# Two sliding-window attentions: the V product no longer stands between the two halves of a step's logits

## The chip, the cores and the metric

The kernel runs on one core of one Trainium2 chip. The metric is device time in microseconds (us) from the start to the end of one execution; a profiled execution also has a span, from its first to its last instruction. The engines are TensorE (PE, with its weight loads PEld), VectorE (DVE), ScalarE (ACT), GpSimd (POOL) and SyncE (SP), which issues most of the DMAs. Each works through its own queue in order and waits on semaphores for the others.

## The reference

Four layers over 2048 rows of 576 values: attention, mixer, attention, mixer. Each adds its result to its input x. Cut to what matters here:

```python
x = x + A(layernorm(x)); x = x + B(layernorm(x)); x = x + A(layernorm(x)); x = x + B(layernorm(x))

def A(x, wqkv, wo):                 # 32 heads of 18 values
    q, k, v = split(x @ wqkv)
    # row s sees the rows s, s-2, ... s-14 (8 of them, those that exist)
    attn = softmax(q . k[window] * 18 ** -0.5)
    return (attn @ v[window]) @ wo

def B(x, w_in, w_sp, b_sp, w_out):  # 4608 = 2 x 2304
    z = gelu(x @ w_in)
    z1, z2 = z[:, :2304], layernorm(z[:, 2304:])
    return (z1 * (w_sp @ z2 + b_sp)) @ w_out
```

## The kernel before, in words

`layer_A` (from L322) is an attention, `layer_B` a mixer. In an attention the order of the work on every engine is written out by hand (`manual_schedule`): engines run their instructions in the order in which the Python code issues them. In the mixers a scheduler places them.

An attention cuts the 2048 rows into 19 tiles t of 112 rows, each with 16 earlier rows as its window's reach. A tile is worked on in two steps, one for each half of the heads, 38 steps s = 2t and 2t + 1 in all. The pieces are:

- `PG`: five products with 512 columns for a piece of Q or K, whose copy goes by DMA to the layout of the logits (`QK`).
- `VW(t, hh, dve)` (L375): the V product, five products of 288 columns for a half of the heads, into a small PSUM tile `pv`, and a cast to `v_ext` on DVE or ACT.
- `L_mm(s)` (L428): 16 logit products, 112 columns, with 32 rows of contraction (18 values of a head and 14 rows that add the mask of the window). They fill two PSUM tiles `L_ps`, `jp` 0 and 1. There are two such buffers, so each belongs to one half of a step (`H_tile`, L199).
- `EXP(s)` (L443): two exponentials on ACT, one per `L_ps` tile.
- `PV(s)` (L451): 16 products of the exponentials with V into one small PSUM tile `O_ps`; then on DVE a reciprocal and a multiplication, the softmax's division; after the second half of the heads a DMA transpose into `oT`.
- `WO(i, hh, c)` (L489): one product of the output projection, 288 columns. Five of them fill a small PSUM tile `pw`, which DVE adds to the old x; after ten, 128 rows are ready and `LN_STATS` (DVE), `LN_XN` (POOL), `XST` and `LN_T` (SP) prepare them for the mixer.

The small tiles `pv`, `O_ps`, `pw` and `pp` share four buffers (`PT_tile`, L202). A buffer is free again when its reader (DVE or ACT) is done.

A table holds for each step which `PG`, `VW` and later work it does. `wo_quota(s)` (L711) reads the table's costs of the step (1.08 us for a `PG`, 0.61 for a `VW`) and fills the step with output products up to 1.28 us of TensorE work in the first attention and 1.33 in the second, at 0.1215 each. What is left over goes to the next step, and `min(7.99, ...)` bounds it. `wo_run(s, n)` (L689) issues up to n of them, as far as the transposed rows are old enough (`wo_from`).

In step s the loop (L737 to L756) issues the logits and exponentials of step s + 1, then `PV(s)`, then the output products that complete a half-filled `pw`, then the table's work, then the rest of the output products. From step 14 (`PG_END`) there is a second form, for a step whose table holds a V product for the first half of the heads: it takes the V product out of the table and issues it between the two halves of the logits of step s + 1:

```python
L_mm(s + 1, (0,))
EXP(s + 1, (0,))
VW(*vws[0][1])
table[s].remove(vws[0])
L_mm(s + 1, (1,))
EXP(s + 1, (1,))
```

These V products are cast on DVE; those of the second half of the heads, in the steps between, are cast on ACT.

Of the kernel before, what the change touches and what calls it, by code (L numbers as in the profile page):

```python
# [62 lines left out]
class K:  # L63
# [258 lines left out]
    def layer_A(self, li):  # L322
# [32 lines left out]
        def tdim(t):  # L355
            nq = min(QT, S - QT * t)
            return HALO + nq, nq
# [11 lines left out]
        def evac(out, in_, dve):  # L369
            if dve:  # L370
                nc.vector.tensor_copy(out=out, in_=in_)  # L371
            else:
                nc.scalar.copy(out=out, in_=in_)

        def VW(t, hh, dve):  # L375
            nk = tdim(t)[0]
            pv = self.PT_tile([P, 512], f32, "pv")
            for c in range(5):
                nc.tensor.matmul(pv[:nk, 0:288], lhsT=self.xnT[:, c, QT * t:QT * t + nk],  # L379
                                 rhs=wv_sb[:, c, hh * 288:(hh + 1) * 288], start=(c == 0), stop=(c == 4))  # L380
            evac(v_ext[:nk, t, 16 * hh:16 * hh + 16, 0:DH], pv[:nk, 0:288].rearrange("p (b d) -> p b d", d=DH), dve)
# [43 lines left out]
        NST = 2 * NT  # L425
        L_tiles = {}

        def L_mm(s, jps=(0, 1)):  # L428
            t, hf = divmod(s, 2)
            nk, nq = tdim(t)  # L430
            if 0 in jps:
                L_tiles[s] = [self.H_tile("L_ps") for _ in range(2)]
            for jp in jps:
                for ftl in range(4):
                    g = 4 * hf + ftl
                    for jj in range(2):
                        j = 2 * jp + jj
                        nc.tensor.matmul(L_tiles[s][jp][:nk, jj, ftl * QT:ftl * QT + nq],  # L438
                                         lhsT=kT[32 * j:32 * j + 32, g, QT * t:QT * t + nk],
                                         rhs=qT[32 * j:32 * j + 32, g, QT * t + PADL:QT * t + PADL + nq],  # L440
                                         start=True, stop=True, tile_position=(32 * j, 0))

        def EXP(s, jps=(0, 1)):  # L443
            nk, nq = tdim(s // 2)
            for jp in jps:
                L_ps = L_tiles[s][jp]
                Lv = L_ps[:, :, 0:4 * QT].rearrange("p a (b c) -> p a b c", c=QT)
                nc.scalar.activation(out=P_bufs[(2 * s + jp) % 4][:nk, :, :, 0:nq], in_=Lv[:nk, :, :, 0:nq], func=ACT.Exp,  # L448
                                     scale=scale)

        def PV(s):  # L451
            t, hf = divmod(s, 2)
            nk, nq = tdim(t)
            O_ps = self.PT_tile([P, 512], f32, "O_ps")
            for jp in range(2):
                for ftl in range(4):
                    for jj in range(2):
                        idx = 4 * ftl + 2 * jp + jj
                        nc.tensor.matmul(O_ps[:, idx * (DH + 1):(idx + 1) * (DH + 1)],  # L459
                                         lhsT=P_bufs[(2 * s + jp) % 4][:nk, jj, ftl, :],  # L460
                                         rhs=v_ext[:nk, t, 16 * hf + idx, :], start=True, stop=True)
            Ov = O_ps[:, 0:16 * (DH + 1)].rearrange("p (h e) -> p h e", e=DH + 1)
            o_t = o_bufs[t % len(o_bufs)]
            rec = sb.tile([P, 16], f32, name="rec", tag="rec", bufs=2)
            nc.vector.reciprocal(out=rec[:nq, :], in_=Ov[:nq, :, DH])
            nc.vector.tensor_tensor(out=o_t[:nq, 288 * hf:288 * (hf + 1)].rearrange("p (h d) -> p h d", d=DH),  # L466
                                    in0=Ov[:nq, :, 0:DH], in1=rec[:nq, :, None].to_broadcast([nq, 16, DH]), op=ALU.mult)
            if hf == 1:
                c0 = (QT * t) % (RING * P)
                if t < NT - 2:  # L470
                    nc.sync.dma_start_transpose(out=oT[:, :, c0:c0 + nq], in_=o_t[:nq, :])
# [194 lines left out]
        table = {}  # L666
# [5 lines left out]
        PG_END = 14  # L672
# [16 lines left out]
        def wo_run(s, n):  # L689

            while n > 0 and wo_pos[0] < 10 * NS:
                i, m = divmod(wo_pos[0], 10)
                if s < wo_from[i]:
                    break
                if m == 0 and i % 2 == 0 and i + 2 < NS:
                    XO(i + 2)
                WO(i, m // 5, m % 5)
                wo_pos[0] += 1
                n -= 1
                if m == 9:  # L700
                    LN_STATS(i)
                    at(s + 1, LN_XN, i)
                    at(s + 1, XST, i)
                    if i < NS - 1:
                        k_ = s + 3
                        if li == 0 and i < 13:
                            k_ = max(k_, 19 + 2 * i if i < 8 else 35 + (i - 8) // 2)
                        at(k_, LN_T, i)
            return n

        def wo_quota(s):  # L711
            if s >= NST:
                return 10 * NS
            used = sum({PG: 1.08, VW: 0.61}.get(f, 0) for f, a in table.get(s, []))
            wo_due[0] = min(7.99, max(0, wo_due[0] % 1 + (wo_fill - used) / 0.1215))
            return int(wo_due[0])
# [10 lines left out]
        for k_, (d, qk, cc) in enumerate(pre):  # L727
            if k_ == (2 if li == 0 else 0):
                L_mm(0)
                EXP(0)  # L730
            PG(d, qk, cc, li > 0 or k_ < 4, q2)
            if li == 0 and k_ == 3:
                self.fill_window_rows(QK, 1)
# [1 line left out]
            VW(nvw - 1, 0, False)  # L735
            VW(nvw - 1, 1, False)
        for s in range(NST):  # L737
            n = wo_quota(s)
            vws = [e for e in table.get(s, []) if e[0] is VW]
            if s >= PG_END and s + 1 < NST - 2 and vws and vws[0][1][1] == 0:  # L740
                L_mm(s + 1, (0,))
                EXP(s + 1, (0,))
                VW(*vws[0][1])
                table[s].remove(vws[0])
                L_mm(s + 1, (1,))
                EXP(s + 1, (1,))
            elif s + 1 < NST:
                L_mm(s + 1)
                EXP(s + 1)
            PV(s)  # L750
            carry = -wo_pos[0] % 5
            n = max(n, carry)
            wo_run(s, carry)
            for f, a in table.pop(s, []):
                f(*a)
            wo_run(s, n - carry)  # L756
        s = NST
# [342 lines left out]
```

## Time and profile before

| | |
|---|---|
| median of 7 executions | 1197.99 us (1193.99 to 1200.7) |
| the profiled execution | 1196.84 us, span 1195.1 us |
| granted TensorE clock, mean | 0.998 |
| first attention, steps 14 to 35 | 77.08 to 126.95 us |
| second attention, steps 14 to 35 | 666.31 to 718.71 us |
| busy in 666.31 to 716.42 (50.11 us) | DVE 40.87, ACT 40.80, POOL 39.15 us |

The chain of work by line, as the page has it, gives the share of the span that each line holds on the path that ended last:

```profile
PE pg L934 41%; PE pz L916 12%; PE po L988 12%; PE pz L837 11%; PE pp L402 5%; PE pv L379 3%; PE pw L498 3%; PE O_ps L459 3%; PE L_ps L438 3%; PE pzs L837 1%; DMA QK<-win2a 1%; POOL QK L77 1%; ACT P_sb L448 0%; DVE ln_st L559 0%; POOL lnx_rstd L565 0%
```

The mixers' lines (pg, pz, po, pzs) hold most of the span. The attentions are the lines pp, pv, pw, O_ps and L_ps. In a timeline a row gives the start (us from the span's start), the duration, the engine, the line, the operation, what it writes and reads, how many instructions are merged in the row, and in brackets how long the engine stood idle before it and for what. "issue" means that the profile shows no other engine as the reason.

### The profile page before, as it was taken

What the parts mean: (1) busy time and instruction counts of PE and PEld (TensorE: products, weight loads), DVE (VectorE), ACT (ScalarE), POOL (GpSimd) and SP (SyncE); (2) the same over time, 40 slices, a digit from 0 to 9 for tenths busy, and PEclk for the clock granted to TensorE, in tenths of its full rate; (3) what the DMA queues carried; (4) which work ended last, traced back from release to release, by engine and by line L of the source; (5) the groups of instructions that cost most, each with busy time, mean ns of one, the idle gap of its engine ahead of it and who ended that gap; (6) DMA issues with size and microseconds to landing.
All of it is one profiled execution on the core that took longest, in us unless ns stands there. A gap on an engine that the chain in (4) does not pass through costs nothing.

```text
span 1195.1 us, 20676 instructions
## 1 busy us (share of the span) xinstructions
PE 1178.3 (99%) x8458; PEld 619.3 (52%) x8554; DVE 546.9 (46%) x1206; ACT 378.0 (32%) x593; POOL 289.4 (24%) x390
## 2 busy tenths in 40 slices
PE   9999999999999999999999999999999999999998
PEld 5566544444444444457755675444444444444676
DVE  9677577333233233244555786863233233232321
ACT  6588667210110110202156886770110110111000
POOL 4777784100000000001153687840000000000000
PEclk9999999999999999999999999999999999999999
DMA  8998892000000000049656799900000000001332
GB/s 199 203 172 184 185 227 51 23 1 12 12 12 12 12 1 12 12 141 288 168 97 115 159 246 208 216 12 11 12 12 1 12 12 12 12 1 35 117 105 73
DMA packets 178190, 101.21 MB, mean 85 GB/s; under 512 B 134501, under 2 KB 159525, under 8 KB 178095
## 3 DMA queue, kind: packets, MB, share of 16 engines
q1 hardware_dynamic: 164943, 77.81, 29.7%
q0 software_dynamic: 6800, 16.32, 5.6%
q10 hardware_dynamic: 6352, 5.75, 1.6%
q8 instruction: 67, 1.10, 0.4%
q14 instruction: 28, 0.23, 0.1%
HBM read 42.39 MB, written 16.53 MB: 49 GB/s over the span
## 4 chain that ended last, share of the span: by engine, by line
PE 95%; DVE 1%; POOL 1%; issue 1%; DMA 1%; ACT 0%; DVEq 0%; ACTq 0%
PE pg L934 41%; PE pz L916 12%; PE po L988 12%; PE pz L837 11%; PE pp L402 5%; PE pv L379 3%; PE pw L498 3%; PE O_ps L459 3%; PE L_ps L438 3%; PE pzs L837 1%; DMA QK<-win2a 1%; POOL QK L77 1%; ACT P_sb L448 0%; DVE ln_st L559 0%; POOL lnx_rstd L565 0%
## 5 line engine op out<-in xcount | busy, mean ns | idle before, releaser
L934 PE MATMUL pg<-Wq,Z 128*128 128x512 bf16 x2256 | 500.3, 379 | 2.5
L934 PEld LDWEIGHTS <-Z 128*128 128x128 bf16 x2304 | 225.2, 98 | 272.1
L938 DVE TENSOR_TENSOR g_tmp<-pg,ln_xn 128x512 f32<-128x512 f32 x144 | 99.6, 691 | 429.2 <-PE pg L934 429.2
L928 ACT ACTIVATE z1T<-pz 128x1024 bf16<-128x1024 f32 x72 | 73.7, 1023 | 513.9 <-PE pz L916 513.7
L77 POOL DMA_DIRECT2D wout<-in_B_w_out_dram x4 | 4.2, 1060 | 604.6 <-PE pg L934 604.6
L448 ACT ACTIVATE P_sb<-L_ps 128x896 bf16<-128x896 f32 (+1 forms) x152 | 129.1, 887 | 40.6 <-PE L_ps L438 38.0
L988 PE MATMUL po<-wout,Z 128*128 128x288 bf16 x1152 | 141.4, 286 | 0.0
L916 PE MATMUL pz<-xnT,w 128*128 128x512 bf16 (+1 forms) x630 | 134.4, 380 | 1.6 <-issue 1.6
L988 PEld LDWEIGHTS <-Z 128*128 128x128 bf16 x1152 | 112.7, 98 | 28.8
L837 PEld LDWEIGHTS <-xnT 128*128 128x128 bf16 (+1 forms) x800 | 66.7, 97 | 84.8 <-issue 28.4
L837 PE MATMUL pz<-win2a,xnT 128*128 128x512 bf16 x366 | 104.8, 384 | 3.2 <-ACT zp L851 2.2
L939 DVE TENSOR_TENSOR Z<-g_tmp,z1T 128x512 bf16<-128x512 f32 x144 | 99.7, 692 | 9.7
L916 PEld LDWEIGHTS <-w 128*128 128x128 bf16 (+1 forms) x640 | 51.0, 97 | 80.1 <-issue 27.1
L402 PE MATMUL pp<-xnT,wqk_sb 128*128 128x512 bf16 x342 | 81.6, 379 | 1.0
L851 ACT ACTIVATE zp<-pz 128x1024 bf16<-128x1024 f32 x64 | 65.5, 1023 | 39.9 <-PE pz L837 30.4
L998 DVE TENSOR_TENSOR x_new<-po,xo 128x288 f32<-128x288 f32 (+1 forms) x64 | 28.8, 455 | 87.6 <-PE po L988 83.4
L837 PE MATMUL pz<-win2b,xnT 128*128 128x512 bf16 (+1 forms) x256 | 66.6, 382 | 0.0
L77 POOL DMA_DIRECT2D QK<-stg x88 | 54.6, 625 | 49.2 <-DVE stg L371 32.9
L379 PE MATMUL pv<-wv_sb,xnT 128*128 128x288 bf16 (+1 forms) x380 | 56.0, 286 | 0.3 <-DVE o_t L466 0.3
L854 DVE CUSTOM_DVE_ANT_0 Z<-zp 128x1536 bf16<-128x1536 bf16 x30 | 52.7, 1758 | 7.2 <-ACT zp L851 7.2
L242 POOL TENSOR_SCALAR ln_xn<-x_new,ln_mv,ln_rstd 128x576 bf16<-128x576 f32 x23 | 54.1, 2351 | 1.9
L402 PEld LDWEIGHTS <-wqk_sb 128*128 128x128 bf16 x360 | 33.3, 97 | 35.9
(117 smaller groups left out, 927.1 us busy)
## 6 DMA issues: line engine op xcount, KB each, us to landing
xres<-x_new SPq DMA_DIRECT2D x48, 288.0 KB
xo<-xres SPq DMA_DIRECT2D x32, 288.0 KB
wout<-in_B_w_out_dram POOLq DMA_DIRECT2D x4, 1296.0 KB, 8.2
xo<-xres SPq DMA_DIRECT2D x8, 576.0 KB
QK<-stg POOLq DMA_DIRECT2D x57, 72.0 KB, 4.8
w<-in_B_w_in_dram SPq DMA_DIRECT2D x16, 256.0 KB
QK<-stg SPq DMA_DIRECT2D x37, 72.0 KB
xo<-in_A_x_dram SPq DMA_DIRECT2D x8, 288.0 KB
```

Of the source, the lines that this page charges most:

```text
L77: return eng.dma_start(out=out, in_=in_)
L379: nc.tensor.matmul(pv[:nk, 0:288], lhsT=self.xnT[:, c, QT * t:QT * t + nk], rhs=wv_sb[:, c, hh * 288:(hh + 1) * 288], start=(c == 0), stop ...
L402: nc.tensor.matmul(pp[:, :], lhsT=w, rhs=self.xnT[:, c, PADL + cc * 512:PADL + (cc + 1) * 512], start=(c == 0), stop=(c == 4))
L448: nc.scalar.activation(out=P_bufs[(2 * s + jp) % 4][:nk, :, :, 0:nq], in_=Lv[:nk, :, :, 0:nq], func=ACT.Exp, scale=scale)
L837: nc.tensor.matmul(pzvs[ci][:, sub * 512:sub * 512 + w], lhsT=self.xnT[r0:r1, c, PADL + i * P:PADL + (i + 1) * P], rhs=win2(c)[r0:r1, c0 + ...
L851: nc.scalar.activation(out=zp[:, c0:c0 + cn], in_=pzvs[ci][:, 0:cn], func=ACT.Gelu_apprx_tanh, accum_out=sums[:, ci:ci + 1])
L916: nc.tensor.matmul(pz1s[q // 2][:, q % 2, :], lhsT=w1[r0:r1, c, sub * P:(sub + 1) * P], rhs=self.xnT[r0:r1, c, PADL + q * 512:PADL + (q + ...
L928: nc.scalar.activation(out=z1T[:, q2 * 512:(q2 + 2) * 512], in_=pz1s[q2 // 2][:, :, :].rearrange("p a b -> p (a b)"), func=ACT.Gelu_apprx_ ...
L934: nc.tensor.matmul(pg[:, :], lhsT=Z[:, jj, i, sub * P:(sub + 1) * P], rhs=Wq[q][:, i, :], start=(i == 0), stop=(i == NS - 1))
L938: nc.vector.tensor_tensor(out=tmp[:], in0=pg[:, :], in1=bsp[:, qs], op=ALU.add)
L939: nc.vector.tensor_tensor(out=uT(jj)[:, sub, qs], in0=tmp[:], in1=z1Ts[jj, sub][:, qs], op=ALU.mult)
L988: nc.tensor.matmul(acc[hh], lhsT=uT(j // 2)[:, j % 2, i * P:(i + 1) * P], rhs=wouts[j // NJH][:, j % NJH, hh * 288:(hh + 1) * 288], start= ...
```

## The change

The second form of the step goes away. `L_mm` and `EXP` lose the parameter that chose a half of the logits, and every step issues all 16 logits and both exponentials before `PV(s)`. The V product stays in the table and is issued there, behind `PV(s)` and the output products that complete a half-filled tile. `wo_quota(s)` is called after `PV(s)` in place of before; it reads the same table entries. The stream of output products itself (`WO`, `wo_run`, `wo_from`, the fill of 1.28 and 1.33) is the same in both kernels.

```diff
-        def L_mm(s, jps=(0, 1)):
+        def L_mm(s):
             t, hf = divmod(s, 2)
             nk, nq = tdim(t)
-            if 0 in jps:
-                L_tiles[s] = [self.H_tile("L_ps") for _ in range(2)]
-            for jp in jps:
+            L_tiles[s] = [self.H_tile("L_ps") for _ in range(2)]
+            for jp in range(2):
...
-        def EXP(s, jps=(0, 1)):
+        def EXP(s):
             nk, nq = tdim(s // 2)
-            for jp in jps:
-                L_ps = L_tiles[s][jp]
+            for jp, L_ps in enumerate(L_tiles.pop(s)):
...
         for s in range(NST):
-            n = wo_quota(s)
-            vws = [e for e in table.get(s, []) if e[0] is VW]
-            if s >= PG_END and s + 1 < NST - 2 and vws and vws[0][1][1] == 0:
-                L_mm(s + 1, (0,))
-                EXP(s + 1, (0,))
-                VW(*vws[0][1])
-                table[s].remove(vws[0])
-                L_mm(s + 1, (1,))
-                EXP(s + 1, (1,))
-            elif s + 1 < NST:
+            if s + 1 < NST:
                 L_mm(s + 1)
                 EXP(s + 1)
             PV(s)
+            n = wo_quota(s)
             carry = -wo_pos[0] % 5
             n = max(n, carry)
             wo_run(s, carry)
             for f, a in table.pop(s, []):
                 f(*a)
             wo_run(s, n - carry)
```

## The prediction

> **What bounds the kernel now.** I read the page's engine shares first, then its chain of work. Two lines carry the reading:
>
> ```profile
> PE 1178.3 (99%) x8458; PEld 619.3 (52%) x8554; DVE 546.9 (46%) x1206; ACT 378.0 (32%) x593; POOL 289.4 (24%) x390
> ...
> PE 95%; DVE 1%; POOL 1%; issue 1%; DMA 1%; ACT 0%; DVEq 0%; ACTq 0%
> ```
>
> TensorE bounds the kernel, and a microsecond less of its time in the attentions is worth nearly a microsecond unless something else is late. Since a busy PE here says little of how dense it is, I next read the timeline of the weight loads, which shows where each block of products begins. This is the second attention, steps 33 and 34 by the order of the program (L438 logits, L459 P times V, L498 output products, L379 V products):
>
> ```profile
> 702.16 0.24 PEld L438 LDWEIGHTS <-QK 32*128 32x128 bf16 x16 [0.24 <-issue]
> 702.49 0.47 PEld L459 LDWEIGHTS <-P_sb 128*128 128x128 bf16 x16
> 702.88 0.10 PEld L498 LDWEIGHTS <-oT 128*128 128x128 bf16 x1
> 702.91 0.58 PEld L379 LDWEIGHTS <-xnT 128*128 128x128 bf16 x5
> 703.52 0.59 PEld L498 LDWEIGHTS <-oT 128*128 128x128 bf16 x5
> 704.34 0.21 PEld L438 LDWEIGHTS <-QK 32*128 32x128 bf16 x8 [0.24 <-issue]
> 704.64 0.48 PEld L379 LDWEIGHTS <-xnT 128*128 128x128 bf16 x5
> 705.36 0.21 PEld L438 LDWEIGHTS <-QK 32*128 32x128 bf16 x8 [0.24 <-issue]
> 705.66 0.47 PEld L459 LDWEIGHTS <-P_sb 128*128 128x128 bf16 x16
> 706.06 0.61 PEld L498 LDWEIGHTS <-oT 128*128 128x128 bf16 x6
> 706.91 0.24 PEld L438 LDWEIGHTS <-QK 32*128 32x128 bf16 x16 [0.24 <-issue]
> ```
>
> The reader is to see two steps with the same work: 16 logits, 16 P-times-V, 5 V products, 6 output products. The whole one runs from 702.16 to 704.34, 2.18 us. The split one runs from 704.34 to 706.91, 2.57 us. Sixteen logits in one block take 0.33 us to the next block (702.16 to 702.49); eight alone take 0.30 (704.34 to 704.64), and a second eight 0.30 again. V products between logits take 0.72 (704.64 to 705.36) and 0.61 elsewhere (702.91 to 703.52). So splitting costs 0.27 + 0.11 = 0.38 us of TensorE, and neither step waits for another engine. The change makes every split step whole.
>
> **What goes, what stays.** I compared the instruction orders engine by engine. On PE only the blocks of the split steps move; on DVE the 20 casts of their V products move behind the normalization of the step (and in most steps behind an addition). ACT, POOL and SP have the same order, so no exponential, DMA or transpose is moved past another. Split steps are those from step 14 with a first-half V product, except near the end: 15, 17, ... 31 in the first attention (9) and 14, 16, ... 34 in the second (11).
>
> Second attention: ten of the eleven take 2.56 to 2.57 us against 2.18 to 2.19 whole: 11 x 0.38 = **4.2 us**. First attention: split steps mostly have five output products and take 2.48 to 2.50 us (106.95 to 109.44, for one). A whole step with six takes 2.18; one product less is 0.12 (a block of six lasts 0.85 to the next block, one of five 0.72), so 2.06: 9 x 0.42 = **3.8 us**. Gross 8.0 us.
>
> **What comes back: the wait for exponentials.** The two logit tiles are double-used: the second half of a step's logits needs the second exponential of the step before to be done. The split hides that wait under the V product; the whole form does not. Its size is in the early steps of the first attention, whose steps are whole and short. First the weight loads, then the timeline of ACT:
>
> ```profile
> 49.07 0.24 PEld L438 LDWEIGHTS <-QK 32*128 32x128 bf16 x16 [0.24 <-issue]
> ...
> 50.99 0.55 PEld L438 LDWEIGHTS <-QK 32*128 32x128 bf16 x16 [0.42 <-issue]
> 51.62 0.47 PEld L459 LDWEIGHTS <-P_sb 128*128 128x128 bf16 x16
> ```
> ```profile
> 49.55 1.73 ACT L448 ACTIVATE P_sb<-L_ps 128x896 bf16<-128x896 f32 x2 [0.57 <-PE L_ps L438]
> 51.46 1.73 ACT L448 ACTIVATE P_sb<-L_ps 128x896 bf16<-128x896 f32 x2 [0.19 <-PE L_ps L438]
> ```
>
> The exponentials start 0.47 us after the first logit load and their pair ends 1.73 later, 2.20 after that load. The next step began 1.92 after it, and its logit block lasted 0.63 instead of 0.33: it ended 2.55 after the earlier step's start. The same sum holds after steps of 2.04, 2.12 and 2.17 us (blocks of 0.51, 0.43, 0.38). So a whole step waits 2.22 - D, where D is the length of the step before it, and nothing if D is longer.
>
> First attention: the formerly split step is 2.06, so the step after it waits 0.16; that one becomes 2.34 and its successor waits nothing. Eight times 0.16 is 1.3. Step 15 follows a step of 1.80 and itself waits 0.42, after which step 16 doesn't wait. Together 1.7: **net 3.8 - 1.7 = 2.1 us**. Second attention: steps of 2.18 wait 0.04 every other time, 21 steps, 0.4; two places follow a 2.06 step (steps 14 and 27), 0.16 each: 0.7. **Net 4.2 - 0.7 = 3.5 us.**
>
> The V cast of the odd steps sits on ACT, 0.41 us. It runs behind the exponentials, from 2.08 to 2.49 after the step's start; the next pair starts at 2.18 + 0.47 = 2.65. It stays covered by 0.16 us. If that cover went, each pair of steps would pay up to 0.41.
>
> **The vector queue and the four small PSUM buffers.** The O tile now takes a buffer before the V tile does. DVE's work is unchanged: 40.87 us in the 50.11 us of the second attention's split steps. In 46.6 us it is 88% busy in place of 82%. Behind the moved cast stand the additions that free output-product tiles; ahead of a normalization stands at times a block of LayerNorm statistics, some 1.2 us from first to last (697.87 to 699.10). One such wait exists now, 0.49 us for a normalization at 117.00. Bounds: 0.5 us better (that wait goes) and 20 x 0.28 = 5.6 worse (what would eat the gain). I take 0, near the whole steps of the trace, which show no DVE wait even when statistics run into them (673.64 and 702.16). The values themselves are used two steps or more later, some 2 us after the cast at worst, and stay covered.
>
> **The way on into the first mixer.** There TensorE stands for 2.3 us and then runs its next twelve products in 4.07 us where the same twelve take 2.27 in other rows, with a granted clock of 0.91 in 140 to 160 us. The chain there shows POOL's z_rstd at 148.02, behind a bias load which waits for the last transposes of the attention:
>
> ```profile
> 147.36 0.64 POOL L77 DMA_DIRECT2D ln_xn<-in_B_b_sp_dram  x1 [5.02 <-DMA xnT<-ln_xn]
> 148.02 0.59 POOL L869 TENSOR_TENSOR z_rstd<-z_rstd,neg_half 128x1 f32<-128x1 f32 x1
> ```
>
> The transposes hang on POOL's LayerNorm work of rows 11 to 15, 124.94 to 142.34, nearly back to back, and that on output products of step 32 and later, behind all split steps. So both sides of the wait move forward together and I take 0. Bounds: if the transposes did not move, the first attention's 2.1 us is lost; if the wait vanished, 2.3 plus 1.8 of slow products is won. The second mixer has no such wait.
>
> **A rule that speaks against.** ACT's records give 4 x 0.87 + 0.41 = 3.9 us per two steps, under the 4.37 of two whole steps, so by the trace evacuation does not decide. The Trainium skill, TensorEngine Tiling (Array Packing), PSUM Bottleneck, says that tiling speeds up TensorE but not the evacuation of PSUM, which may then bound the work. Were logits and exponentials in series, two steps would take 2 x 2.20 + 0.41 = 4.81 against 4.76 now, and in place of a gain each pair of steps of the second attention would lose 0.05.
>
> **Sum.** 2.1 + 3.5 = 5.6 us off the profiled execution's 1196.84 (span 1195.1): 1191.2. That execution is 1.15 under the median of seven, 1197.99; on the median it gives **1192.4 us**.
>
> **Rivals.**
> - *The exponentials take it back* (0.12). The ACT cast or a later start puts some 0.4 us on each of 20 pairs: 8.2 against 8.0 gross, no gain, about 1198; half of it gives 1194 to 1196. For: the cover is only 0.16 us. Against: in the split pairs of now, exponentials behind the cast wait for logits, not the reverse.
> - *DVE becomes the bound* (0.06): slower. The P-times-V product waits for a buffer held behind statistics and the moved cast. At the 0.49 us seen once, 20 times, 9.8 - 5.6 = 4.2 worse: 1202. It decides from 0.28 us per split step. For: 88% busy. Against: no such wait in the whole steps.
> - *The first mixer absorbs the first attention's part* (0.12): 1194.5.
> - *More than forecast* (0.12): the mixer's wait shrinks or the small waits don't come: 1188 to 1190.
> - *The change does not do what it says*: its name speaks of a stream of output products, and that stream is in both kernels; the quota moves but reads the same table, and the counts are equal. If only that counted, the time would not change. The split's removal is real in the PE order, so I give this no chance.
>
> **Chances.** The forecast holds 0.58, within some 2 us. A measurement of this kernel can tell 0.3%, 3.6 us, from no change. Faster: 0.58 + 0.12 (more than forecast) + 0.07 of the mixer case = 0.77. Same: 0.12 (exponentials) + 0.05 = 0.17. Slower: 0.06. The range runs from 1187.5 (gross 8.0 plus most of the wait) to 1197.0 (the exponentials take nearly all); it leaves out the slower case and the tails.
>
> **What would show it.** Right: in the weight loads no block of eight logits is left from step 14 on; formerly split steps last about 2.06 (first) and 2.19 us (second); logit blocks of 0.48 after them in the first attention and 0.33 to 0.37 in the second; the second attention's last whole step begins some 5.6 us earlier. Wrong: logit blocks of 0.7 us and more in most steps (exponentials), P-times-V or V loads that wait for DVE over and over (buffers), or a wait near 148 us grown by 2 us (mixer). A V product that keeps its 0.72 us between output products would cost 20 x 0.11, 2.2 us of the gain.

## The result, and the profile after

The changed kernel takes 1191.44 us (median of 18 executions, 1189.43 to 1197.1), the kernel before 1197.72 beside it (47 executions, 1193.69 to 1201.58). The ratio is 0.9953, with a 95% interval of 0.9943 to 0.9962: 6.3 us faster by the medians. Two further series of the same kernel on other chips gave 0.9963 (0.9949 to 0.9977) and 0.9964 (0.9949 to 0.9979), 5.2 and 4.8 us.

The profiled execution of the changed kernel is its slowest, 1197.1 us with a span of 1195.3, so its span cannot be set against that of before. It lost time where the change does not reach: a Q/K product that starts at 54.15 us had waited 4.2 us for a transpose of x. Its page says so, in the engine shares and in the chain of work:

```profile
PE 1174.5 (98%) x8458; PEld 619.7 (52%) x8554; DVE 545.7 (46%) x1206; ACT 375.8 (31%) x593; POOL 293.9 (25%) x390
...
PE 93%; DMA 3%; issue 1%; POOL 1%; SPq 1%; DVE 1%; ACT 1%; POOLq 0%; DVEq 0%; ACTq 0%
```

The instruction counts are those of before, PE is 3.8 us less busy, and DMA has 3% of the chain in place of 1%. What the change did has to be read step by step. The timeline of the weight loads in the second attention, steps 29, 30 and 31 (L437 logits, L457 P times V, L496 output products, L379 V products):

```profile
700.22 0.24 PEld L437 LDWEIGHTS <-QK 32*128 32x128 bf16 x16 [0.24 <-issue]
700.55 0.47 PEld L457 LDWEIGHTS <-P_sb 128*128 128x128 bf16 x16
...
702.41 0.27 PEld L437 LDWEIGHTS <-QK 32*128 32x128 bf16 x16 [0.24 <-issue]
702.77 0.47 PEld L457 LDWEIGHTS <-P_sb 128*128 128x128 bf16 x16
703.17 0.49 PEld L379 LDWEIGHTS <-xnT 128*128 128x128 bf16 x5
703.68 0.71 PEld L496 LDWEIGHTS <-oT 128*128 128x128 bf16 x6
704.63 0.24 PEld L437 LDWEIGHTS <-QK 32*128 32x128 bf16 x16 [0.24 <-issue]
...
705.75 0.59 PEld L379 LDWEIGHTS <-xnT 128*128 128x128 bf16 x5
708.11 0.11 PEld L496 LDWEIGHTS <-oT 128*128 128x128 bf16 x2 [1.77 <-DMA oT<-o_t]
```

Step 30 was split before and lasted about 2.57 us. Now it is one block of 16 logits and then the rest, 702.41 to 704.63, 2.22 us; its logit block takes 0.36. The last line is new: in step 31 an output product waits 1.77 us for the transposed rows `oT`. No such wait stood in the second attention before.

The same view in the first attention, steps 25 to 27:

```profile
106.93 0.24 PEld L437 LDWEIGHTS <-QK 32*128 32x128 bf16 x16 [0.24 <-issue]
107.25 0.47 PEld L457 LDWEIGHTS <-P_sb 128*128 128x128 bf16 x16
...
108.99 0.39 PEld L437 LDWEIGHTS <-QK 32*128 32x128 bf16 x16 [0.24 <-issue]
109.48 0.47 PEld L457 LDWEIGHTS <-P_sb 128*128 128x128 bf16 x16
...
111.34 0.24 PEld L437 LDWEIGHTS <-QK 32*128 32x128 bf16 x16 [0.24 <-issue]
```

The formerly split step lasts 2.06 us, and the one behind it 2.35, because its logit block takes 0.49 in place of 0.33: the wait for exponentials.

Read from such views (us): from the start of step 14 to that of step 35 in each attention, and from the last output product of the first attention to the first gate product (`pg`) of the mixer behind it. What the three columns and the time up to step 14 leave of the span agrees within 1.6 us (939.0 to 940.6). Ahead of step 14 the start of the program varies (step 14 begins at 77.08 us in before, at 82.69 in the changed kernel's profile).

| profile | first attention | second attention | way into the mixer | span |
|---|---|---|---|---|
| before | 48.39 | 50.11 | 80.31 | 1195.1 |
| before_again_1 | 48.38 | 50.90 | 77.75 | 1196.3 |
| before_again_2 | 48.37 | 50.11 | 80.39 | 1198.0 |
| changed | 46.09 | 49.72 | 77.28 | 1195.3 |
| after_again | 46.08 | 48.15 | 78.32 | 1189.4 |
| after_third | 46.05 | 47.96 | 77.39 | 1188.2 |
| first_whole | 46.08 | 50.63 | 78.27 | 1191.2 |
| second_whole | 48.39 | 46.87 | 77.87 | 1190.3 |
| split_pv | 47.65 | 50.03 | 77.71 | 1194.5 |
| whole_v_early | 46.18 | 47.95 | 80.19 | 1190.8 |
| short_exp | 43.84 | 47.97 | 77.89 | 1188.5 |
| row11_later | 46.06 | 48.61 | 77.53 | 1189.9 |
| xn_later | 46.05 | 48.83 | 78.32 | 1191.7 |
| short_store | 46.05 | 46.73 | 77.51 | 1188.8 |

With the same code the first attention repeats within 0.04 us. The second, and the way into the mixer, do not.

### The profile page after: what moved, and what is told of

Same layout as the page of the kernel before. It is cut to its first block, busy times and chain, and to the rows that moved or that the text cites. A ratio compares the mean times of both kernels' runs of the same rounds, so it can differ in the third digit from the quotient of the medians.

```text
span 1195.3 us, 20676 instructions
## 1 busy us (share of the span) xinstructions
PE 1174.5 (98%) x8458; PEld 619.7 (52%) x8554; DVE 545.7 (46%) x1206; ACT 375.8 (31%) x593; POOL 293.9 (25%) x390
## 4 chain that ended last, share of the span: by engine, by line
PE 93%; DMA 3%; issue 1%; POOL 1%; SPq 1%; DVE 1%; ACT 1%; POOLq 0%; DVEq 0%; ACTq 0%
PE pg L924 41%; PE pz L906 12%; PE po L978 12%; PE pz L827 10%; PE pp L402 5%; PE pw L496 3%; PE pv L379 3%; PE O_ps L457 3%; PE L_ps L437 2%; PE pzs L827 1%; DMA xnT<-ln_xn 1%; POOL QK L77 1%; DMA wqk_sb<-in_A_wqkv_dram 1%; DMA oT<-o_t 1%; SPq L77 0%
## 5 line engine op out<-in xcount | busy, mean ns | idle before, releaser
L446 ACT ACTIVATE P_sb<-L_ps 128x896 bf16<-128x896 f32 (+1 forms) x152 | 126.6, 887 | 45.6 <-PE L_ps L437 45.2
L379 PE MATMUL pv<-wv_sb,xnT 128*128 128x288 bf16 (+1 forms) x380 | 56.5, 288 | 0.0
L496 PE MATMUL pw<-wo_sb,oT 128*128 128x288 bf16 x320 | 54.5, 288 | 1.5 <-DMA oT<-o_t 1.5
```

The source lines that it names most:

```text
L496: nc.tensor.matmul(pw[:, 0:288], lhsT=oT[:, c, r0:r0 + P], rhs=wo_sb[:, c, hh * 288:(hh + 1) * 288], start=(c == 0), stop=(c == 4))
```

## The experiments

The theory at this point: the halved logit block costs 0.38 to 0.42 us per step; making it whole brings back the wait for exponentials, 2.22 - D; the transfers of the second attention take part of the rest. Rivals: the V product's place gives the gain, not the logits; something outside the attentions does.

### One attention at a time: first_whole and second_whole

Made from the kernel before: the split is kept in the second attention alone, or in the first alone.

```diff
-            if s >= PG_END and s + 1 < NST - 2 and vws and vws[0][1][1] == 0:
+            if li > 0 and s >= PG_END and s + 1 < NST - 2 and vws and vws[0][1][1] == 0:   # first_whole
+            if li == 0 and s >= PG_END and s + 1 < NST - 2 and vws and vws[0][1][1] == 0:  # second_whole
```

> The first attention has whole steps, the second keeps the split of before. Theory (the split itself costs 0.38 to 0.42 us of TensorE per step, and the wait for exponentials gives some back): formerly split steps of 2.06 us and followers of 2.34 in the first attention, 2.57 still in the second; 2.1 to 2.4 us less than before, ratio about 0.998. Rival (the gain comes from the first mixer, whose wait near 148 us shrinks when its inputs come earlier): 4 to 6 us less, all of the change's gain.

> The second attention has whole steps, the first keeps the split of before. Theory: steps of 2.19 to 2.22 us in place of 2.57; 3.5 to 4.2 us less than before, ratio about 0.9968; with the kernel that has only the first attention whole, the two gains add up to the change's 6.3. Rival (the first mixer): little, 0 to 2 us, since nothing ahead of that mixer differs.

Measured: first_whole 1194.54 us, ratio 0.9967 (0.9953 to 0.9982); second_whole 1194.99, 0.9976 (0.9962 to 0.9989). The first attention alone becomes 2.30 us shorter, the second alone 3.24 us (50.11 to 46.87), with no wait of TensorE for a DMA in it. In these profiles the two add up to 5.5 us. The medians give 2.6 and 2.2 us; the second is below the 3.5 to 4.2 that was expected, with an interval of 1.3 to 4.6.

### Half the logits, but no V product between them: split_pv

Made from the kernel before: the split steps issue half the logits, `PV(s)`, the other half, and the V product where the changed kernel has it.

```diff
             if s >= PG_END and s + 1 < NST - 2 and vws and vws[0][1][1] == 0:
                 L_mm(s + 1, (0,))
                 EXP(s + 1, (0,))
-                VW(*vws[0][1])
-                table[s].remove(vws[0])
+                PV(s)
                 L_mm(s + 1, (1,))
                 EXP(s + 1, (1,))
-            elif s + 1 < NST:
-                L_mm(s + 1)
-                EXP(s + 1)
-            PV(s)
+            else:
+                if s + 1 < NST:
+                    L_mm(s + 1)
+                    EXP(s + 1)
+                PV(s)
```

> Both attentions: the logits of the formerly split steps stay in two halves, but the P-times-V products of the step stand between them and not the V product; the V product and its cast stand where the change puts them. Theory (halved logits cost 0.27 us and the turn to and from them 0.11): the steps stay at about 2.57 us and the time is that of before, ratio 0.999 to 1.001. Rival (the gain comes from where the V product and its cast stand, which frees the small buffers and the vector queue): the time of the change, ratio 0.995.

Measured: 1194.91 us, 0.998 (0.9967 to 0.9993). The weight loads of one such step of the first attention:

```profile
85.74 0.21 PEld L438 LDWEIGHTS <-QK 32*128 32x128 bf16 x8 [0.24 <-issue]
86.05 0.51 PEld L459 LDWEIGHTS <-P_sb 128*128 128x128 bf16 x16
86.58 0.21 PEld L438 LDWEIGHTS <-QK 32*128 32x128 bf16 x8
86.89 0.36 PEld L498 LDWEIGHTS <-oT 128*128 128x128 bf16 x4
87.27 0.59 PEld L379 LDWEIGHTS <-xnT 128*128 128x128 bf16 x5
87.88 0.10 PEld L498 LDWEIGHTS <-oT 128*128 128x128 bf16 x1
88.22 0.24 PEld L438 LDWEIGHTS <-QK 32*128 32x128 bf16 x16 [0.24 <-issue]
```

Each half costs 0.31 us whatever stands between them, and now P times V takes 0.53 (86.05 to 86.58) where it takes 0.40 between other products. The step lasts 2.48 us, as when split by a V product. The first attention gains 0.73 us, of which 0.49 is the normalization's buffer wait at 117.00 that is gone; the second gains 0.08. The line of before in which that wait stands:

```profile
117.00 0.49 PEld L379 LDWEIGHTS <-xnT 128*48 128x48 bf16 x5 [0.49 <-DVE o_t L466]
```

The median lies 2.3 us below before's, where no gain was expected. Some 1.5 us of that are not explained by the attentions; the interval allows a gain of only 0.8.

### Whole logits, but the V product early: whole_v_early

Made from the kernel before: the V product keeps its place ahead of `PV(s)`, behind 16 logits in one block.

```diff
-                L_mm(s + 1, (0,))
-                EXP(s + 1, (0,))
+                L_mm(s + 1)
+                EXP(s + 1)
                 VW(*vws[0][1])
                 table[s].remove(vws[0])
-                L_mm(s + 1, (1,))
-                EXP(s + 1, (1,))
```

> All 16 logits stand in one block, but the V product and its cast stay early: behind the logits and ahead of P times V. Theory (halving the logits is what cost): steps as in the changed kernel, 2.06 and 2.19 us plus waits, 5 to 6.5 us less than before, ratio 0.9953. Rival (the early V product and its cast cost, through the small buffers or the vector queue): the time of before, or at most half of the gain.

Measured: 1194.12 us, 0.9971 (0.9956 to 0.9985). Steps as in the changed kernel, here one of the second attention:

```profile
677.64 0.24 PEld L438 LDWEIGHTS <-QK 32*128 32x128 bf16 x16 [0.25 <-issue]
677.97 0.48 PEld L379 LDWEIGHTS <-xnT 128*128 128x128 bf16 x5
678.47 0.58 PEld L459 LDWEIGHTS <-P_sb 128*128 128x128 bf16 x16
678.98 0.61 PEld L498 LDWEIGHTS <-oT 128*128 128x128 bf16 x6
679.83 0.27 PEld L438 LDWEIGHTS <-QK 32*128 32x128 bf16 x16 [0.24 <-issue]
```

2.19 us from 677.64 to 679.83. With split_pv this completes a square: split or whole, V early or late. Both whole forms have short steps and both split forms long ones, so it is the halving that makes a step long, and the V product's place does not. The whole executions do not say it as clearly. The median is 3.1 us below before's, where 5 to 6.5 were expected, and 2.1 us above the changed kernel's on the same chip (after_again, 1192.04; the intervals of the two ratios overlap), though the first attention is only 0.1 longer; the profile shows 80.19 in the way into the mixer. So some 2 us of the total may go with the V product's place, as in split_pv, but outside the steps.

### Half the exponentials: short_exp

Made from the changed kernel: from step 15 each exponential covers half of its columns, so half of that work of ACT is left out.

```diff
+                ne = nq if s < 15 else nq // 2
-                nc.scalar.activation(out=P_bufs[(2 * s + jp) % 4][:nk, :, :, 0:nq], in_=Lv[:nk, :, :, 0:nq], func=ACT.Exp,
+                nc.scalar.activation(out=P_bufs[(2 * s + jp) % 4][:nk, :, :, 0:ne], in_=Lv[:nk, :, :, 0:ne], func=ACT.Exp,
```

> The changed kernel, but from step 15 on the exponentials cover only the first half of a tile's columns (half of the work of ACT there is left out, and the rest of the products use old values). Theory (after the change whole steps wait 2.22 us less the length of the step before, for the exponentials): the logit blocks of 0.48 and 0.36 us go down to 0.33, 2.4 to 3.4 us less than the changed kernel, about 1188.5, ratio to before 0.9925. Rival (the blocks are long for another reason, such as the turn of the array or the small buffers): no less than the changed kernel, ratio 0.995.

Measured: 1190.27 us, 0.995 (0.9932 to 0.9969). The weight loads of the same steps 25 and 26 of the first attention as above:

```profile
102.51 0.24 PEld L437 LDWEIGHTS <-QK 32*128 32x128 bf16 x16 [0.38 <-issue]
102.84 0.47 PEld L458 LDWEIGHTS <-P_sb 128*128 128x128 bf16 x16
...
104.58 0.24 PEld L437 LDWEIGHTS <-QK 32*128 32x128 bf16 x16 [0.24 <-issue]
104.90 0.47 PEld L458 LDWEIGHTS <-P_sb 128*128 128x128 bf16 x16
...
106.76 0.24 PEld L437 LDWEIGHTS <-QK 32*128 32x128 bf16 x16 [0.24 <-issue]
```

The logit blocks are back at 0.33 and 0.32 us, where the second had 0.49, and the steps last 2.07 and 2.18. The first attention becomes 2.24 us shorter than in the changed kernel: the longer blocks were the exponentials. The total would not have told it: 0.995 is the rival's ratio. The gain over before of 6.9 us is only 0.6 to 2.1 more than in the three series of the changed kernel, where 2.4 to 3.4 were expected; in this profile a wait of 1.2 us that ends at 74.19 and one of 1.4 us in the second attention (a V product whose buffer an addition still holds) stand against it.

### Does the second attention's wait come back? after_again, before_again_1, before_again_2, after_third

The changed kernel and the kernel before, unaltered.

> The changed kernel once more, for its times beside those of the others and for a second profile. Theory: the first attention from step 14 to 35 lasts 46.1 us against 48.4 before, the second 46.8 against 50.1, so 5.6 us less by the attentions, ratio 0.9953; a wait for a transposed tile as in the first profile (1.77 us) comes by chance and is not there again at the same place. Rival (the change makes the transposes late): the wait is at the same place again.

> The kernel before, for a second profile. Theory: its steps last what they lasted (48.4 us and 50.1 us for steps 14 to 35), and the first mixer's stretch from the end of the output products to its first gate product, 80.31 us in the first profile of before against 77.3 to 78.3 in the other kernels, changes from run to run whatever the kernel. Rival (the mixer's wait hangs on the attention's form): 80 us again.

> The kernel before a third time, for the same question: does the first mixer's stretch stay at 80 us or change from run to run between 77 and 80.

> The changed kernel again, on the same chip as the two with later rows. Theory: ratio 0.995 to 0.996, the second attention's steps 14 to 35 between 46.9 and 49.7 us, with the wait for the transposed tile in step 31 again or nearly again.

Measured: after_again 1192.04 us, 0.9963; before_again_1 1198.07 and before_again_2 1199.81, one execution each; after_third 1192.01, 0.9964. In after_again the output product of step 31 waits again, 1.51 us. In after_third step 31 does not wait, but another chain does. The waits of all engines in its second attention (engine and line, for whom, us in total, times, longest):

```profile
DVE x_new L500 <- DMA xo<-xres: 1.7, 2, 1.4
...
PE pv L379 <- DVE x_new L500: 0.8, 1, 0.8
```

The old rows `xo` land late, the addition waits for them, the small PSUM tile it reads stays taken, and a V product waits for that buffer. In before_again_1 and before_again_2 no product of the second attention's steps 14 to 35 waits for a DMA directly. But the same chain stands in before_again_1: an addition waits 1.82 us for `xo`, an output product 0.42 behind it, and the second attention takes 0.8 us longer. Late transfers are there with split steps too.

The way into the mixer is 77.75 in one of the two and 80.39 in the other, so it varies without any change to the code.

### Which transfer is late: row11_later and xn_later

Both from the changed kernel. row11_later lets the output products of one row block start one step later, xn_later issues the transposes for the mixer two steps later, so that they no longer stand ahead of `oT` in SP's queue. SP's timeline in the changed kernel had suggested both:

```profile
697.58 1.24 SPq L249 DMA_TRANSPOSE xnT<-ln_xn  x1
698.91 0.84 SPq L77 DMA_DIRECT2D xo<-xres  x1
699.86 1.30 SPq L469 DMA_TRANSPOSE oT<-o_t  x1
```

The third line is the transpose that TensorE waits for until 708.11, 8.25 us from its issue.

```diff
+            if li > 0 and t == 13:          # row11_later
+                wo_from[-1] += 1
...
-                        k_ = s + 3
+                        k_ = s + (5 if li > 0 and i < 11 else 3)   # xn_later
```

> The changed kernel, but in the second attention the output products of row tile 11 may start at step 32 at the earliest in place of 31. In two profiles of the changed kernel TensorE waits 1.5 to 1.8 us in step 31 for the transposed tile that this row reads; before, with longer steps, it never did. Theory (four steps of 2.2 us are too few for a transpose that lands late in a crowded DMA queue): no wait for a transposed tile, second attention from step 14 to 35 near 46.9 us in place of 48.2 to 49.7, total 0.5 to 1.8 us less than the changed kernel. Rival (the transposes are late by more than a step, or the wait moves to another DMA): the wait is in step 32 or later, and the total is the changed kernel's.

> The changed kernel, but in the second attention the transposes of the normalized rows 0 to 10 are issued two steps later, so that SP does not stand waiting for GpSimd's row while a finished attention tile waits behind it. Theory (the tile is late because SP issues it late, behind a waiting row): its issue comes right after the division, no wait in step 31, second attention near 46.9 us, total 0.5 to 1.8 us less than the changed kernel. Rival (it is late because the DMA engines are full): the wait stays.

Measured: row11_later 1191.81 us, 0.9958 (0.9943 to 0.9972); xn_later 1192.42, 0.9965 (0.9946 to 0.9984). In row11_later the wait for `oT` is gone, but the second attention is no shorter (48.61): P times V now waits for PSUM buffers, 0.4 to 0.6 us at a time. In xn_later additions wait for `xo`, 2.5 us in two times, and the second attention takes 48.83. So neither a step that comes too early nor the order of SP's queue is the cause by itself: with one wait removed, another came.

### Fewer bytes: short_store

Made from the changed kernel. The second attention stores 72 of 576 columns of its result, so 4.1 MB of stores are left out; the rest of that buffer is filled once, in the first mixer, with older values.

```diff
-            self.dma(self.xres[li][i * P:(i + 1) * P, :], tails[i]["x"][:])
+            ns = D if li == 0 else 72
+            self.dma(self.xres[li][i * P:(i + 1) * P, 0:ns], tails[i]["x"][:, 0:ns])
...
+            if li == 1 and jj == 2:
+                self.dma(self.xres[2][:, 72:D], self.xres[0][:, 72:D], eng=nc.sync)
```

> The changed kernel, but the second attention stores only 72 of the 576 columns of its result; the rest of that buffer is filled once during the first mixer from an older buffer, so the last mixer adds old values there. About 4.1 MB of stores leave the crowded 50 us. Theory (in the whole-step kernels the second attention meets waits of 1 to 3 us for a transposed tile or for x because the DMA engines are full there): no such wait, steps 14 to 35 near 46.9 us in place of 48.0 to 49.7, total 1 to 2 us less than the changed kernel. Rival (the waits come from SP's order or from the latency of a transfer, not from the amount): waits as before, 48 us and more.

Measured: 1190.88 us, 0.994 (0.9927 to 0.9954). The second attention takes 46.73 us and its weight loads wait for no DMA:

```profile
PEld L437 <- issue: 5.2, 22, 0.2
PEld L496 <- issue: 0.2, 1, 0.2
PEld L457 <- DVE o_t L464: 0.2, 1, 0.2
```

What the DMA queue held (packets, MB, share of 16 engines; the shares of a window can add up to more than 100%). First before, in 666 to 717 us, then the changed kernel in the same stretch, then after_again and short_store in 662 to 711:

```profile
q1 hardware_dynamic: 15879, 9.85, 93.1%
```
```profile
q1 hardware_dynamic: 16031, 10.01, 95.9%
```
```profile
q1 hardware_dynamic: 15393, 9.60, 98.8%
```
```profile
q1 hardware_dynamic: 16687, 7.33, 86.5%
```

The queue was near full before the change, the two profiles of the changed kernel show more, and short_store less, with 2.3 MB less in the stretch. That fits the theory but does not show it. second_whole stores everything, and no product of its second attention waits for a DMA either: 46.87 us. Its queue in 690 to 712:

```profile
q1 hardware_dynamic: 8756, 5.25, 111.0%
```

In the changed kernel, with its wait of 1.77 us, the share in the same stretch is 112.2%, in short_store 99.8%. In xn_later, whose additions wait 2.5 us, it is 92.8% in 663 to 712, below before's 93.1. So the share does not tell which profile waits. Of the eight profiles with whole steps and all stores in the second attention seven take 1.1 to 2.9 us more than 46.8, one does not; a single short_store without waits may be such a one. Its total does not decide either: its interval overlaps the changed kernel's.

## Why the prediction was right, point by point

- *What bounds the kernel.* Right: TensorE. The attentions' steps alone gave 5.5 us where nothing else was late.
- *The split costs 0.38 and 0.42 us.* Right, to some 0.02: the whole steps last 2.06 and 2.19, as forecast. (Not ten but nine of the eleven split steps of the second attention took 2.56 or 2.57; the others took 2.44 and 2.62, which hardly moves the sum.) split_pv and whole_v_early show that the two blocks of eight are the cost, 0.31 each in place of 0.33 for all sixteen, with 0.11 to 0.13 more for the block that stands between them. The kernel issues the first half at the array's row positions 0 and 32, the second at 64 and 96; that the halves run side by side only in a whole block would fit these times, but no run tests it.
- *The wait for exponentials, 2.22 - D.* Right in rule and size: logit blocks of 0.48 or 0.49 behind steps of 2.06 (0.48 by the rule), 0.36 behind steps of 2.19 (0.36). Step 24, behind a step of 1.58, has 0.97 (104.09 to 105.06), and 0.33 + 2.22 - 1.58 is 0.97; the forecast had not listed that step, but 0.30 us of the wait stood there before as well. Five blocks of the changed kernel's profile are 0.03 to 0.18 us longer than the rule gives, one of them in the stretch of lower clock behind step 31. short_exp halved the exponentials, and every block of the first attention from step 15 to 34 was back at 0.32 or 0.33.
- *First attention 2.1 us.* Measured 2.30. The forecast's bound "0.5 better (that wait goes)" is in it: the 0.49 at 117.00 is gone in the changed kernel and in split_pv. Without it the steps gave 1.8, 0.3 less than the sum.
- *Second attention 3.5 us.* The price of the steps was right: 3.24 in second_whole. But the three profiles of the changed kernel average 48.6 against 50.4 of before's three, a gain of 1.8. **This is the step that failed:** the comparison of orders ended with "no exponential, DMA or transpose is moved past another", and the transfers were put at nothing on that ground. The order did stay. But TensorE came to its products sooner, and in three profiles of three a late `oT` or `xo` stopped it: 1.5 us between the price and the average gain. With split steps such a delay shows in two profiles of five (before_again_1 and first_whole, 0.8 and 0.5 us longer), so late transfers are not new with the change; TensorE has less time ahead of it when they come. The prediction read no DMA share of the stage, which was 93.1% before. What makes a transfer late, and whether fewer bytes would cure it, stays open.
- *DVE and the four small buffers, 0.* Right by themselves: in second_whole and short_store a single wait of 0.2 us. Where `xo` makes an addition late, a buffer is late too, which is DMA again. In after_third, row11_later and xn_later a P-times-V product also waits some 0.5 us for a normalization; what held that up was not traced.
- *The way into the mixer, 0.* Not met in the profiles. The way takes 77.3 to 80.4 us; the three profiles of before average 79.5, the three of the changed kernel 77.7, 1.8 less, as much as the second attention lost against its price (3.24 - 1.76 = 1.5). All 14 profiles follow one wait of TensorE, for ACT to empty the mixer's PSUM tile into `zp`. Here it is in before and in the changed kernel:

```profile
152.75 1.44 PE L837 MATMUL pz<-win2a,xnT 128*128 128x512 bf16 x3 [2.16 <-ACT zp L851]
```
```profile
154.67 0.81 PE L827 MATMUL pz<-win2a,xnT 128*128 128x512 bf16 x3 [0.78 <-ACT zp L841]
```

  In the eleven profiles where this wait is 0.78 to 1.82 us, the way lasts 76.5 us and the wait. In the three where it is 2.05 to 2.40 (before, before_again_2, whole_v_early) it is 1.5 to 1.7 us more, and the granted clock behind the wait is 0.59 to 0.63. The chain that the forecast named is the right one: POOL's bias load, behind the last transposes, starts 12.1 to 13.7 us after the last output product, and the wait is in every profile that time less 11.3. So "both sides of the wait move forward together" does not hold: their distance differs by up to 1.6 us from profile to profile. Whether the change shortens it is not shown. Where the V product stands early in the first attention, three profiles of five reach 80 us, where it stands late none of nine, but the waits of the two groups overlap (1.25 to 2.40 and 0.78 to 1.82), and before_again_1 shows 77.75 with the code of before.
- *The rule that speaks against.* The Trainium skill, TensorEngine Tiling (Array Packing), PSUM Bottleneck, warns that emptying PSUM may come to bound tiled products. In these runs it bounds in part: a step that shares its two logit tiles with the next cannot be followed sooner than 2.22 us. In series, as the forecast's other sum had it, two steps would take 4.81; a pair in the second attention takes 4.41 (2.19 + 2.22).
- *The sum.* 5.6 us forecast; 6.3, 5.2 and 4.8 measured in three series. In the profiles the parts are 2.3, 1.8 and, in the way into the mixer, 1.8, where 2.1, 3.5 and 0 were forecast. One term was too large by 1.7 us and another too small by as much: that the total was met so well is in part luck, and proves less than the steps do.
- *Rivals.* The exponentials took back their forecast share and no more; DVE did not become the bound; the mixer did not absorb the first attention's part (first_whole is 2.6 us faster in all).

No kernel of the experiments that does the whole work beats the changed one by more than the intervals.

## What to carry to other kernels

A small product block cut in two can cost more than its instruction count says: compare whole blocks in the timeline, start to start, before and behind the cut. When a double-used buffer sets a smallest interval between steps, take it from the trace as one number (here 2.22 us) and apply it to each step's length; it forecast nearly every block. And a faster engine leaves less time to everything it waits for: ask how long before their use the transfers are issued in the stage that gets shorter, not only whether their order stays, and take a few profiles where waits move from run to run, since one may show the stage without them.

## What the runs showed of the hardware

Eight logit products in a block take nearly as long as sixteen: 0.30 or 0.31 us to the next block, against 0.33.

A short stop of TensorE can cost more than itself. In step 31 of the changed kernel its products stand for 1.47 us (the weight loads for 1.77), and the granted clock behind that is 0.70 for 5 us. The window's columns are the stretch and its length, the busy time of PE, PEld, DVE, ACT and POOL, the granted clock, the DMA share and GB/s:

```profile
708.00:713.00 5.00, 4.88 (x81) 3.25 (x82) 3.42 (x11) 2.80 (x4) 3.09 (x3) 0.70 1.08 336
```

In before, behind the 2.16 us that end at 152.75 in the mixer, it is 0.60:

```profile
152.75:156.90 4.15, 4.15 (x14) 1.27 (x14) 3.37 (x9) 2.46 (x7) 3.30 (x3) 0.60 0.99 146
```

Behind the 2.05 and 2.40 us of whole_v_early and before_again_2 at the same place it is 0.59 and 0.63. Behind the 1.78 and 1.82 us of first_whole, after_again and xn_later there, and behind the 1.21 us of step 31 in after_again, it stays at 1.00. So the length of a stop alone does not decide it here. The Trainium skill, TensorE: Matmul & The Clock Gate, Part 1: The HAM clock gate, gives an idle window of some 3.4 us as what lowers the clock; here stops of 1.5 to 2.4 us were followed by a lower one, so by the measurement that figure is no safe bound.

A transpose by DMA on a queue that is over 90% taken came into use 8.25 us after its issue, and which transfer was late changed between profiles of the same kernel.
